# Router parts at two places of a token tile, and list products as one operation a part

## The chip, the cores and the metric

The kernel runs on one core of a Trainium2 chip. TensorE (PE in the profile) multiplies matrices, VectorE (DVE), ScalarE (ACT) and GpSimd (POOL) work on elements, and SyncE (SP) issues most transfers. Each engine runs its own queue of instructions in order and waits on semaphores. The metric is the device time of one execution in microseconds (us); the median of several runs counts.

## The reference

Sliding-window attention is followed by a mixture of experts with one expert a token:

```python
q, k, v: (8, 8, 576, 64); window 64, causal
scores = where(mask, q @ k.T / 8, -1e9)
attn = softmax(scores); x = (attn @ v) as (4608, 512)
do_compute = x @ w_skip > 0
logits = x[do_compute] @ w_gate                 # 8 experts
e = argmax(logits); gate = softmax(logits)[e]
y = gate * (relu(x @ w1[e]) @ w2[e])            # w1 (512, 1024), w2 (1024, 512)
out = x, and x + y where do_compute
```

## The kernel before

The 4608 tokens are 36 tiles of 128. One loop with the tile number t from 0 to 36 runs the attention as a pipeline: in step t TensorE gets the scores of tile t+1 (`ps`), products that prepare the gate (`pw`, `pk`), in steps 32 and 33 the transposes of the first expert's tokens (`px`), then `av` of tile t-2 and the transposes of tile t-1 (`pt`). VectorE does the softmax of tile t (`soften`: `mx`, `s`, and the exponential on ScalarE), then the normalisation of tile t-2 (`tile_out`: `r`, `x`, `lh`; `lh` holds the parts of the gate's logits). ScalarE copies the transposes to `ptm`, which `av` needs. The whole order is written out by hand: each engine takes its instructions in the order in which the code issues them.

The router works on groups of tiles (`GRP`: 8, 8, 6, 8, 4 and 2 tiles). `route` is a generator that issues the work of a group in parts: the logits `lg`, `gmx` and `gd`, `gfi` and `gfm`, `goh` and `gohb` (which expert each token takes, as one-hot rows), then the sums over tokens on TensorE, `pr`, with `gds` and `base` on VectorE, then `gnd`, `gs`, `gate`, `pos`, `low`, `posp`, and on POOL the one-hot rows `hot`. `routes` takes it a part further, so many parts as its first argument says; a part that follows "sums" is held back until it has been asked for three times, and `routes(1, False)` does not issue it. `pt`, `pw`, `pk`, `pr`, `pe` and the experts' `p` share two PSUM buffers of the tag "t".

After 22 tiles (`NCLOSE`) the generator also closes the first lists: `close_first` picks the two experts with the most tokens (`perm`, from which SyncE loads the first weights), `entries` makes the lists of their first tokens, `es0` (`es` in the profile), and POOL gathers those tokens to the four `xg` of the first two experts.

`entries` builds a list as a product of one-hot matrices: for a step of tiles VectorE compares positions (`of`), POOL multiplies the result with five rows of values (`ofv`), TensorE sums over tokens (`pe`, or `peu` for the late lists), and VectorE turns the sums into indices and gates (`raw_e`, then `es0` or `les`).

After the loop the experts run in blocks of products (`p` is a block of 12 with 256 columns, `yw` and `yv` one of 12 with 512) while the last groups are routed. Weights arrive as `raw`, and are split into `whi` (ScalarE) and `wlo` (VectorE); ScalarE and VectorE turn a `p` into `hh` and `hl`. When the router is done, `order_experts` (from `c` on) and `late_lists` make the late lists in nine steps of four tiles; `PACE` says how many parts of `late_lists` are issued before each expert block. From `les` POOL gathers the next tokens (`xg`), which TensorE transposes to `px`, and a finished `yo` goes out by a scatter on POOL.

Of the kernel before, what the change touches and what calls it, by code (L numbers as in the profile page):

```python
# [13 lines left out]
ALU = mybir.AluOpType  # L14
# [5 lines left out]
P = 128  # L20
# [19 lines left out]
NCLOSE = 22  # L40
# [9 lines left out]
USPLIT = (35,)  # L50
RATE = 1

PACE = 4

XSPLIT = (32, 33)

# [68 lines left out]
def window_attention_moe(ctx: ExitStack, tc, a, out):  # L125
    nc = tc.nc
# [26 lines left out]
    vals = const.tile([P, 5, NT], BF16, name="vals")  # L153
# [90 lines left out]
    def soften(t):  # L244
        ps = ss[t]
        s = sp.tile([P, 2 * 4, P], F32, name="s")
        flat = ps.rearrange("p r h k -> p (r h) k")
        mx = sm.tile([P, 8], F32, name="mx", bufs=2)
        nc.vector.tensor_reduce(mx, flat, axis=AX.X, op=ALU.max)  # L249
        nc.vector.tensor_tensor(s, flat, mx.unsqueeze(2).to_broadcast([P, 8, P]), op=ALU.subtract)  # L250
        nc.scalar.activation(s, s, AF.Exp, scale=0.125)  # L251
        ss[t] = s
# [214 lines left out]
    def entries(ts, starts, le, pool, since, take, step, lag):  # L467


        nc_ = starts.shape[1]  # L470
        parts(slice(since, ts.stop))
        yield
        pe, built = None, []
        for t0 in range(ts.start, ts.stop, step):
            m = min(step, ts.stop - t0)
            tj = slice(t0, t0 + m)
            of = pool.tile([P, m, nc_], BF16, name="of", bufs=1 if take is psum else 3)
            nc.vector.tensor_tensor(
                of,
                posp[:, tj].unsqueeze(2).to_broadcast([P, m, nc_]),  # L480
                starts.unsqueeze(1).to_broadcast([P, m, nc_]),
                op=ALU.is_equal,
            )
            ofv = pool.tile([P, m, 5, nc_], BF16, name="ofv", bufs=1 if take is psum else 3)
            for v in range(5):
                nc.gpsimd.tensor_tensor(  # L486
                    ofv[:, :, v], of, vals[:, v, tj].unsqueeze(2).to_broadcast([P, m, nc_]), op=ALU.mult
                )
                if v in (1, 3):
                    yield  # L490
            built.append((t0, ofv))
            yield "sums" if take is psum else None
            if len(built) < lag and t0 + step < ts.stop:
                continue
            if pe is None:
                pe = (
                    psum.tile([P, 5, nc_], F32, name="pe", tag="t", bufs=2, padded_shape=[P, 5, 100])
                    if take is psum
                    else banks["late"].tile([P, 5, nc_], F32, name="peu", tag="u", bufs=1, padded_shape=[P, 5, 100])
                )  # L500
            while built and (len(built) >= lag or t0 + step >= ts.stop):
                first_t, ofs = built.pop(0)
                for j in range(ofs.shape[1]):
                    t = first_t + j
                    nc.tensor.matmul(pe, hot[:, t], ofs[:, j], start=t == ts.start, stop=t == ts.stop - 1)
                yield
        entry(pe, le, pool)
        yield
# [65 lines left out]
    held = [None, 0]  # L574

    def routes(n, sums=True):

        for _ in range(n):
            if not late:
                return  # L580
            if held[0] == "sums":
                held[1] += 1
                if not sums or held[1] < 3:
                    continue
            held[:] = next(late[0], late), 0
            if held[0] is late:
                late.pop(0)
# [52 lines left out]
    def weight_dma_first():  # L640
        weight_dma(ptr["dma"])
        ptr["dma"] += 1
# [189 lines left out]
    with tc.manual_schedule():  # L832
# [35 lines left out]
        for t in range(NT + 1):  # L868
            m, r = divmod(t, 9)
            for f, n in at.get(t, ()):  # L870
                f(n)
            if t + 1 < NT:
                score(t + 1)
            for f, n in gate_at.get(t, ()):
                f(n)
            rest = its[0].split(*xhl[0], XSPLIT.index(t), "t") if t in XSPLIT else None
            routes(1)
            if t < NT:
                soften(t)
            if t >= 2 and t < NT:  # L880
                tile_out(t - 2)
            if rest is not None:
                rest()
            routes(1, False)
            if t >= 1 and t < NT:
                transpose_p(t - 1)
            routes(1 if t < NCLOSE else 2)
            for f, n, j in lower_at.get(t, ()):
                f(n, j)
            for _ in range(U0.count(t)):  # L890
                weight_dma_first()
            if t in USPLIT:
                weight_split(ptr["split"])
                ptr["split"] += 1
# [181 lines left out]
        while True:  # L1076
# [4 lines left out]
            if tabling is not None:  # L1081
                next(tabling, None)
            for _ in range(PACE):
                next(listing, None)
# [92 lines left out]
```

## Time and profile before

| | before |
|---|---|
| median of 3 runs | 467.93 us (466.89 to 470.29) |
| profiled execution | 465.82 us |
| its span in the profile | 464.0 us |
| TensorE busy | 411.8 us (89%) |
| VectorE busy | 308.3 us (66%) |
| ScalarE busy | 218.4 us (47%) |
| POOL busy | 125.6 us (27%) |

The span is the stretch of the trace from the first to the last instruction of the program; the execution's own time is 1.8 us more. The busy shares are means over stages that differ: the attention loop lasts until about 183 us, the experts' products from there to the end.

### The profile page before, as it was taken

What the parts mean: (1) busy time and instruction counts of PE and PEld (TensorE: products, weight loads), DVE (VectorE), ACT (ScalarE), POOL (GpSimd) and SP (SyncE); (2) the same over time, 40 slices, a digit from 0 to 9 for tenths busy, and PEclk for the clock granted to TensorE, in tenths of its full rate; (3) what the DMA queues carried; (4) which work ended last, traced back from release to release, by engine and by line L of the source; (5) the groups of instructions that cost most, each with busy time, mean ns of one, the idle gap of its engine ahead of it and who ended that gap; (6) DMA issues with size and microseconds to landing.
All of it is one profiled execution on the core that took longest, in us unless ns stands there. A gap on an engine that the chain in (4) does not pass through costs nothing.

```text
span 464.0 us, 11417 instructions
## 1 busy us (share of the span) xinstructions
PE 411.8 (89%) x4568; PEld 342.9 (74%) x4568; DVE 308.3 (66%) x609; ACT 218.4 (47%) x365; POOL 125.6 (27%) x188
## 2 busy tenths in 40 slices
PE   2899989979779967894899999999999999999983
PEld 2577767867567756783689888898888789988762
DVE  2478989989788988687533658947355566756420
ACT  1387667767546755462312534434243445444410
POOL 2311215116052505246860402405007030101010
PEclk9999999999898998996999999999999999999998
DMA  7999989949847943556533561845537456656100
GB/s 245 394 351 401 384 284 404 398 127 390 356 146 250 355 128 112 151 196 207 174 111 100 184 207 69 277 137 185 193 114 250 161 197 198 216 193 219 51 29 20
DMA packets 35096, 99.31 MB, mean 214 GB/s; under 512 B 4480, under 2 KB 6528, under 8 KB 35040
## 3 DMA queue, kind: packets, MB, share of 16 engines
q1 hardware_dynamic: 31840, 88.97, 55.8%
q0 software_dynamic: 3200, 9.58, 5.8%
q8 instruction: 37, 0.61, 0.5%
q14 instruction: 19, 0.16, 0.1%
HBM read 84.46 MB, written 14.39 MB: 213 GB/s over the span
## 4 chain that ended last, share of the span: by engine, by line
PE 64%; DVE 9%; ACT 3%; DMA 3%; POOL 2%; issue 1%; POOLq 0%; DVEq 0%; SPq 0%; ACTq 0%
PE p L695 8%; PE p L697 8%; PE p L696 8%; PE av L344 4%; PE yw L695 3%; PE yw L697 3%; PE yw L696 3%; PE yv L695 3%; PE yv L696 3%; PE yv L697 3%; PE pt L260 3%; PE ps L234 3%; POOL ofv L486 2%; DMA vm<-vp 2%; DVE s L250 2%; PE px L684 2%
## 5 line engine op out<-in xcount | busy, mean ns | idle before, releaser
L648 DVE TENSOR_TENSOR wlo<-raw,whi 128x1024 fp32r<-128x1024 f32 x72 | 88.1, 1229 | 15.4 <-ACT whi L647 15.4
L732 ACT ACTIVATE hh<-p 128x256 fp32r<-128x256 f32 (+6 forms) x72 | 27.7, 384 | 146.6 <-PE p L697 145.6
L697 PE MATMUL p<-xh,wlo 128*128 128x256 f32 (+6 forms) x288 | 84.2, 292 | 1.6 <-DVE wlo L648 1.6
L695 PE MATMUL p<-xh,whi 128*128 128x256 f32 (+6 forms) x288 | 85.3, 296 | 0.3 <-ACT ptm L261 0.3
L696 PE MATMUL p<-xl,whi 128*128 128x256 f32 (+6 forms) x288 | 84.1, 292 | 0.0
L733 DVE SCALAR_TENSOR_TENSOR hl<-p,hh 128x256 fp32r<-128x256 f32 (+6 forms) x72 | 30.3, 420 | 76.8 <-ACT hh L732 76.7
L647 ACT CAST whi<-raw 128x1024 fp32r<-128x1024 f32 x72 | 74.2, 1046 | 0.0
L755 POOL DMA_INDIRECT out<-yo,les x18 | 18.9, 1052 | 156.0 <-DVE yo L754 144.1
L695 PEld LDWEIGHTS p<-xh,whi 128*128 128x128 f32 x288 | 55.0, 191 | 3.4 <-ACT ptm L261 0.4
L251 ACT ACTIVATE s<-s 128x1024 f32<-128x1024 f32 x36 | 38.1, 1058 | 40.3 <-DVE s L250 38.1
L697 PEld LDWEIGHTS p<-xh,wlo 128*128 128x128 f32 x288 | 55.1, 191 | 2.0 <-DVE wlo L648 2.0
L696 PEld LDWEIGHTS p<-xl,whi 128*128 128x128 f32 x288 | 55.1, 191 | 1.4
L249 DVE TENSOR_REDUCE mx<-ps 128x8 f32<-128x1024 f32 x36 | 43.8, 1215 | 15.0 <-PE ps L234 15.0
L250 DVE TENSOR_TENSOR s<-ps,mx 128x1024 f32<-128x1024 f32 x36 | 44.1, 1225 | 5.1 <-PE pt L260 0.9
L260 PE MATMUL pt<-ident,s 128*128 128x128 f32 x288 | 41.0, 284 | 5.6 <-ACT ptm L261 5.6
L344 PEld LDWEIGHTS av<-vm,ptm 128*64 128x64 f32 x1024 | 36.1, 138 | 11.4 <-issue 5.7
L344 PE MATMUL av<-vm,ptm 128*64 128x74 f32 x1024 | 41.3, 233 | 2.2 <-ACT ptm L261 2.1
L315 POOL COPY vm<-vm 64x1184 f32<-64x1184 f32 x16 | 18.6, 1168 | 88.5 <-ACT vm L314 61.0
L234 PE MATMUL ps<-k,q 64*64 64x128 f32 x1024 | 37.3, 285 | 4.1 <-DMA q<-qT 4.1
L261 ACT COPY ptm<-pt 128x512 f32<-128x512 f32 x72 | 38.6, 580 | 4.7 <-PE pt L260 4.5
L260 PEld LDWEIGHTS pt<-ident,s 128*128 128x128 f32 x288 | 31.5, 143 | 9.8 <-ACT ptm L261 6.5
L234 PEld LDWEIGHTS ps<-k,q 64*64 64x64 f32 x1024 | 33.1, 142 | 7.2 <-DMA k<-kT 4.4
(173 smaller groups left out, 697.5 us busy)
## 6 DMA issues: line engine op xcount, KB each, us to landing
raw<-wq SPq DMA_DIRECT2D x72, 512.0 KB, 4.4
vm<-vp SPq DMA_DIRECT2D x16, 592.0 KB, 6.8
vT<-vT SPq DMA_DIRECT2D x16, 512.0 KB, 7.6
out<-x SPq DMA_DIRECT2D x32, 256.0 KB, 6.3
q<-qT SPq DMA_DIRECT2D x15, 512.0 KB, 9.0
k<-kT SPq DMA_DIRECT2D x8, 640.0 KB, 6.8
k<-kT SPq DMA_DIRECT2D x7, 512.0 KB, 8.3
kt<-kT SPq DMA_DIRECT2D x8, 256.0 KB, 7.6
```

Of the source, the lines that this page charges most:

```text
L234: nc.tensor.matmul(ps[64 * hf : 64 * hf + 64, r, p], q[h, p], k[h, :, p], start=False, stop=p == 3, skip_group_check=True,)
L249: nc.vector.tensor_reduce(mx, flat, axis=AX.X, op=ALU.max)
L250: nc.vector.tensor_tensor(s, flat, mx.unsqueeze(2).to_broadcast([P, 8, P]), op=ALU.subtract)
L251: nc.scalar.activation(s, s, AF.Exp, scale=0.125)
L260: nc.tensor.transpose(pt[:, p], s[:, 4 * r + p], ident)
L261: nc.scalar.copy(ptm[:, 4 * r : 4 * r + 4], pt)
L344: nc.tensor.matmul(av[64 * hf : 64 * hf + 64, h // 4, (h % 4) * VW : (h % 4 + 1) * VW], ptm[:, (h % 2) * 4 + h // 2, 64 * hf : 64 * hf + 6 ...
L647: nc.scalar.copy(hi, raw)
L648: nc.vector.tensor_tensor(lo, raw, hi.bitcast(F32), op=ALU.subtract)
L695: nc.tensor.matmul(o, lh, rh, start=first, stop=False)
L696: nc.tensor.matmul(o, lh, rl, start=False, stop=False)
L697: nc.tensor.matmul(o, ll, rh, start=False, stop=last)
```

## The change

In the attention loop the router's parts are issued at other places. Before, each step t had one `routes` ahead of the softmax, one (that never issues the sums) behind the normalisation, and one behind the transposes (two from tile 22 on). Now there is one between softmax and normalisation and one behind the transposes, and from tile 22 on one more ahead of the softmax. A held part is issued at the second call instead of the third.

In `entries` the five products of a step, one for each row of values, become one operation with five times as many elements, and the two parts that lay between them are gone. `PACE` goes from 4 to 3.

```diff
--- before.py
+++ after.py
@@ -50,7 +50,7 @@
 USPLIT = (35,)
 RATE = 1
 
-PACE = 4
+PACE = 3
 
 XSPLIT = (32, 33)
 
@@ -482,12 +482,12 @@
                 op=ALU.is_equal,
             )
             ofv = pool.tile([P, m, 5, nc_], BF16, name="ofv", bufs=1 if take is psum else 3)
-            for v in range(5):
-                nc.gpsimd.tensor_tensor(
-                    ofv[:, :, v], of, vals[:, v, tj].unsqueeze(2).to_broadcast([P, m, nc_]), op=ALU.mult
-                )
-                if v in (1, 3):
-                    yield
+            nc.gpsimd.tensor_tensor(
+                ofv,
+                of.unsqueeze(2).to_broadcast([P, m, 5, nc_]),
+                vals[:, :, tj].rearrange("p v t -> p t v").unsqueeze(3).to_broadcast([P, m, 5, nc_]),
+                op=ALU.mult,
+            )
             built.append((t0, ofv))
             yield "sums" if take is psum else None
             if len(built) < lag and t0 + step < ts.stop:
@@ -580,7 +580,7 @@
                 return
             if held[0] == "sums":
                 held[1] += 1
-                if not sums or held[1] < 3:
+                if not sums or held[1] < 2:
                     continue
             held[:] = next(late[0], late), 0
             if held[0] is late:
@@ -874,17 +874,18 @@
             for f, n in gate_at.get(t, ()):
                 f(n)
             rest = its[0].split(*xhl[0], XSPLIT.index(t), "t") if t in XSPLIT else None
-            routes(1)
+            if t >= NCLOSE:
+                routes(1)
             if t < NT:
                 soften(t)
+            routes(1)
             if t >= 2 and t < NT:
                 tile_out(t - 2)
             if rest is not None:
                 rest()
-            routes(1, False)
             if t >= 1 and t < NT:
                 transpose_p(t - 1)
-            routes(1 if t < NCLOSE else 2)
+            routes(1)
             for f, n, j in lower_at.get(t, ()):
                 f(n, j)
             for _ in range(U0.count(t)):
```

The instructions themselves stay the same but for the list products; the order on the engines moves. On TensorE, in the attention loop, the sums `pr` of the first group stand here before (`pw` and `pk` prepare the gate, `av` is the product with the values, `pt` the transposes, `ps` the scores):

```order
L294 MATMUL pw<-vT,wg 32x256 x4
L344 MATMUL av<-vm,ptm 64x74 x16
L260 MATMUL pt<-ident,s 128x128 x8
L410 LDWEIGHTS trib
L410 MATMUL pr<-gohb,trib 128x64
L413 LDWEIGHTS onesb
L413 MATMUL pr<-gohb,onesb 128x64
L413 LDWEIGHTS onesb
L413 MATMUL pr<-gohb,onesb 128x56
```

There they follow the transposes at once. In the changed kernel they stand here on TensorE:

```order
L220 LDWEIGHTS identb
L220 MATMUL ps<-band,identb 64x512
L220 LDWEIGHTS identb
L220 MATMUL ps<-band,identb 64x512
L234 MATMUL ps<-k_112,q 64x128 x16
L302 MATMUL pk<-ident,vw_1014 128x128 x2
L410 LDWEIGHTS trib
L410 MATMUL pr<-gohb,trib 128x64
L413 LDWEIGHTS onesb
L413 MATMUL pr<-gohb,onesb 128x64
```

The sums moved from directly behind the transposes to behind the next tile's scores and `pk`; those of the second and third group move in the same way, and those of the fourth stay directly behind the transposes.

On VectorE, among the first expert blocks, the choice of the experts of the fifth group (four tiles, 32 columns: `gohb`) stood between the first `wlo` and the normalisation of the last tile but one:

```order
L648 TENSOR_TENSOR wlo_134<-raw_128,whi_133 128x1024
L398 SCALAR_TENSOR_TENSOR gfi<-gd,cf 128x32
L400 TENSOR_REDUCE gfm<-gfi 128x4
L405 TENSOR_TENSOR goh<-gfi,gfm 128x32
L407 SCALAR_TENSOR_TENSOR gohb<-lg,goh 128x32
L353 TENSOR_SCALAR r<-av 128x8
L354 RECIPROCAL r<-r 128x8
L355 TENSOR_TENSOR x<-av,r 128x512
L361 TENSOR_TENSOR lh<-av,r 128x8x9
L648 TENSOR_TENSOR wlo_136<-raw_129,whi_135 128x1024
L733 SCALAR_TENSOR_TENSOR hl<-p_3186,hh 128x256
L422 TENSOR_TENSOR gds<-pr,base 128x32
```

All of it was issued before the first `hl` of an expert block. In the changed kernel it stands, on the same engine, behind two `wlo` and the `hl` of the fourth expert block:

```order
L648 TENSOR_TENSOR wlo_3104<-raw_130,whi_3103 128x1024
L648 TENSOR_TENSOR wlo_3106<-raw_131,whi_3105 128x1024
L733 SCALAR_TENSOR_TENSOR hl<-p_3288,hh 128x256
L386 TENSOR_REDUCE lg<-lh 128x36
L393 TENSOR_REDUCE gmx<-lg 128x4
L395 TENSOR_TENSOR gd<-lg,gmx 128x32
L398 SCALAR_TENSOR_TENSOR gfi<-gd,cf 128x32
L400 TENSOR_REDUCE gfm<-gfi 128x4
L405 TENSOR_TENSOR goh<-gfi,gfm 128x32
L407 SCALAR_TENSOR_TENSOR gohb<-lg,goh 128x32
L733 SCALAR_TENSOR_TENSOR hl<-p_3321,hh 128x256
L422 TENSOR_TENSOR gds<-pr,base 128x32
```

All parts of this group moved behind the start of the experts' products; on TensorE its sums stand behind the fifth block of `p` where they stood behind the first. Those of the sixth group (16 columns) stood behind six blocks of `p` and one of `yw`, and stand now behind eight of `p` and one and a half of `yw`.

On VectorE, at the end of the late lists, `raw_e` (which reads the sums of the lists) stood ahead of the two `yo` and of the next `hl`:

```order
L478 TENSOR_TENSOR of<-posp,begins 128x72
L733 SCALAR_TENSOR_TENSOR hl<-p_3710,hh 128x256
L478 TENSOR_TENSOR of<-posp,begins 128x72
L513 COPY raw_e<-peu 128x90
L514 SCALAR_TENSOR_TENSOR raw_e<-raw_e 128x18
L515 TENSOR_SCALAR les<-raw_e 128x18
L516 TENSOR_TENSOR raw_e<-raw_e 128x18
L517 TENSOR_TENSOR les<-raw_e 128x18
L754 SCALAR_TENSOR_TENSOR yo<-yw,es_119,xg_120 128x512
L754 SCALAR_TENSOR_TENSOR yo<-yw,es_119,xg_121 128x512
L733 SCALAR_TENSOR_TENSOR hl<-p_3790,hh 128x256
```

Nothing lay between the last `of` and `raw_e`. In the changed kernel it stands, on the same engine, behind two `yo` and an `hl`:

```order
L648 TENSOR_TENSOR wlo_3108<-raw_132,whi_3107 128x1024
L478 TENSOR_TENSOR of<-posp,begins 128x72 x3
L754 SCALAR_TENSOR_TENSOR yo<-yw,es_119,xg_120 128x512
L754 SCALAR_TENSOR_TENSOR yo<-yw,es_119,xg_121 128x512
L733 SCALAR_TENSOR_TENSOR hl<-p_3729,hh 128x256
L513 COPY raw_e<-peu 128x90
L514 SCALAR_TENSOR_TENSOR raw_e<-raw_e 128x18
L515 TENSOR_SCALAR les<-raw_e 128x18
L516 TENSOR_TENSOR raw_e<-raw_e 128x18
L517 TENSOR_TENSOR les<-raw_e 128x18
L733 SCALAR_TENSOR_TENSOR hl<-p_3756,hh 128x256
```

So `les` comes one expert block later against the last sums; the scatters of the two `yo` stand ahead of the gathers by `les` on POOL, where they stood behind them. The first late sums `peu` on TensorE come two blocks of `p` and one of `yw` later than before, and those of two steps stand there together.

In the attention loop the first lists (`es0`) come out one tile later: ahead of the row maximum of tile 31, where they came ahead of that of tile 30. The transposes `px` that take the first gathered tokens stand in step 32 as before.

## Rows read from the trace of the kernel before

**Rows 1.** Busy time of each engine by stage; then granted clock, DMA share, GB/s.

```profile
14.00:183.00 169.00, 147.74 (x2884) 116.59 (x2876) 143.68 (x306) 109.40 (x191) 50.58 (x79) 0.97 0.83 302
...
209.60:238.00 28.40, 18.32 (x124) 15.70 (x124) 16.79 (x43) 6.14 (x11) 20.93 (x48) 0.82 0.50 158
238.00:456.00 218.00, 215.92 (x1304) 185.42 (x1302) 123.12 (x195) 87.09 (x141) 41.45 (x36) 1.00 0.50 163
```

**Rows 2.** Waits, TensorE and VectorE 10 to 184 us, TensorE 183 to 250.

```profile
PE pr L410 <- ACT ptm L261: 5.3, 3, 3.0
...
DVE gds L422 <- PE pr L413: 3.3, 4, 0.9
...
PE peu L505 <- POOL ofv L486: 9.8, 4, 6.9
```

**Rows 3.** Timeline of VectorE in the attention loop: start, us, operation [idle before].

```profile
123.48 0.21 DVE L422 TENSOR_TENSOR gds<-pr,base 128x48 f32<-128x48 f32 x1 [0.88 <-PE pr L413]
...
127.96 0.17 DVE L353 TENSOR_SCALAR r<-av 128x8 f32<-128x8 f32 x1 [1.43 <-PE av L344]
...
166.78 0.23 DVE L422 TENSOR_TENSOR gds<-pr,base 128x64 f32<-128x64 f32 x1 [0.76 <-PE pr L413]
```

**Rows 4.** Timeline of TensorE: the scores of two tiles.

```profile
123.80 1.92 PE L234 MATMUL ps<-kt,qt 64*64 64x128 f32 x32
...
158.42 1.04 PE L234 MATMUL ps<-k,q 64*64 64x128 f32 x32
```

**Rows 5.** Timelines of POOL, VectorE and TensorE around the first gather.

```profile
150.64 1.25 POOL L524 DMA_INDIRECT xg<-out,es  x1 [6.13 <-DVE raw_e L516]
...
154.46 1.22 DVE L249 TENSOR_REDUCE mx<-ps 128x8 f32<-128x1024 f32 x1
...
160.25 0.66 PE L684 MATMUL px<-ident,xg 128*128 128x128 f32 x4
```

**Rows 6.** DMA issues, 150 to 151.5 us: the gather, us from issue to landing.

```profile
xg<-out,es POOLq DMA_INDIRECT x1, 7.5
```

**Rows 7.** Timeline of VectorE: parts of the router's fifth group.

```profile
180.88 0.45 DVE L386 TENSOR_REDUCE lg<-lh 128x36 f32<-128x288 f32 x1
...
181.59 0.19 DVE L395 TENSOR_TENSOR gd<-lg,gmx 128x32 f32<-128x32 f32 x1
```

**Rows 8.** Timeline of TensorE around the late lists.

```profile
216.74 0.46 PE L505 MATMUL peu<-ofv,hot 128*128 128x90 bf16 x4 [6.91 <-POOL ofv L486]
216.99 0.56 PE L695 MATMUL p<-xh,whi 128*128 128x256 f32 x1
...
219.70 0.52 PE L505 MATMUL peu<-ofv,hot 128*128 128x90 bf16 x4
...
234.52 0.28 PE L695 MATMUL p<-xh,whi 128*128 128x256 f32 x1
...
235.94 0.28 PE L695 MATMUL p<-xh,whi 128*128 128x256 f32 x1
...
237.78 0.63 PE L684 MATMUL px<-ident,xg 128*128 128x128 f32 x4 [0.26 <-DMA xg<-out,les]
```

**Rows 9.** List products: ns min/median/max; then the mean of a smaller product.

```profile
L486 POOL TENSOR_TENSOR ofv<-of,vals x50: 300/307/1357, 141.6 to 232.5; 128x72 bf16<-128x72 bf16 x45, 128x88 bf16<-128x88 bf16 x5
...
L463 POOL TENSOR_TENSOR left<-gate,vals 128x22 f32<-128x22 f32 x1 | 0.2, 233 | 0.1
```

**Rows 10.** Timeline of VectorE around the late lists.

```profile
208.47 0.15 DVE L952 TENSOR_TENSOR c<-base,cf 128x8 f32<-128x8 f32 x1
...
213.27 1.22 DVE L648 TENSOR_TENSOR wlo<-raw,whi 128x1024 fp32r<-128x1024 f32 x1
...
233.25 0.25 DVE L513 COPY raw_e<-peu 128x90 f32<-128x90 f32 x1 [1.93 <-PE peu L505]
...
234.04 0.18 DVE L517 TENSOR_TENSOR les<-raw_e 128x18 f32<-128x18 f32 x1
...
236.56 0.42 DVE L733 SCALAR_TENSOR_TENSOR hl<-p,hh 128x256 fp32r<-128x256 f32 x1 [1.01 <-ACT hh L732]
```

## Prediction

> **What bounds the kernel now.** I read the stages first, then who waits, then the timeline at the places that the change touches. Up to 183 us VectorE is busy 143.68 of 169.00 us and TensorE 147.74; from 238 us on TensorE is busy 215.92 of 218.00 us at full clock [rows 1]. So whatever time is won or lost before 238 us is kept to the end: behind it there is no slack to lose it in. Between them the late lists are built (209.6 to 238 us): TensorE is busy only 18.32 of 28.40 us there, and its granted clock is 0.82 of full speed, a mean over stretches at 2.4 GHz and one below [rows 1]. The change acts on four places: the waits around the router's sums in the attention loop, the first gather, the sums of the last two router groups among the first expert products, and the late lists. Each is priced against the profiled execution (465.82 us); the median of the runs, 467.93 us, lies 2.1 us above it.
>
> **The attention loop: 3.3 us less.** VectorE waits four times for `pr`, 3.3 us in all; TensorE itself waits three times before `pr` for the copy that frees the buffer of the tag that `pr` shares, 5.3 us in all [rows 2]. The 0.76 us at 166.78 is that of the fourth group [rows 3], whose `pr` still stands directly behind the transposes; that stays. The other three (3.3 - 0.76 = 2.55 us) belong to `pr` standing directly behind the transposes, with the scores of the next tile behind it. Now those scores come first and cover the wait of the shared buffer. The worst of them, 3.0 us, also left TensorE slow: the 32 products of the next score took 1.92 us, where 1.04 us is the rule [rows 4], and VectorE then waited 1.43 us for `av` [rows 3]. I take the three waits whole and half of the 1.43 us, since the buffer's wait does not vanish, it moves to `pk` or `pw` ahead of `pr`: -3.3 us. Bounds: -4.0 us (all of it) and -1.0 us, because `pr` now stands ahead of `av`, and a late `gohb` would hold `av` and with it VectorE's next `r`. The group's parts lie further apart in the tiles, but they are as many operations as before.
>
> **The first gather: 1.9 us more.** With one router step a tile fewer, the first lists come out one tile later: `es` stood ahead of the row maximum of tile 30, now it stands ahead of that of tile 31. The gather that follows `es` was issued at 150.64 and landed 7.5 us later [rows 5, 6], at 158.1 us; TensorE took it into `px` at 160.25 without a wait [rows 5]. Tile 30 ended at 154.46 [rows 5]. One tile later the gather is issued at about 154.6 and lands at 162.1 us, 1.9 us after `px` is due, and `px` stands ahead of `av` on TensorE. The queue of `px` has `av`, the transposes and the next scores behind it, so VectorE waits too. Taken: 1.9 us. Bounds: 0 (a landing in 5.6 us) to 3.5 us (tile 30 longer than before by the router parts that move into it).
>
> **Sums of the last two groups: 3.8 us more.** The sums of the fifth group (32 columns) stood behind one expert block; now they stand behind four more, and ahead of them on VectorE is a row: `hl` of one block, two `wlo`, `hl` of the next, then seven small operations from `lg` to `gohb`. A block of 12 products lasts 235.94 - 234.52 = 1.42 us [rows 8]; its `hl` is done 236.56 + 0.42 - 235.94 = 1.04 us after its end [rows 8, 10]; a `wlo` takes 1.22 us [rows 10]; `lg` takes 0.45 us and the next operations follow some 0.22 us apart [rows 7], together about 1.8 us. So `gohb` is ready 1.04 + 2.4 + 0.42 + 1.8 = 5.7 us after the end of the first of these blocks, and TensorE has two blocks, 2.84 us, until it wants it: 2.9 us of wait. If the two `wlo` are done early, it is 1.04 + 1.8 - 1.42 = 1.4 us. I take 1.8 us, nearer to the lower end, since an earlier wait for a `wlo` is part of the longer one and exists today. Those of the sixth group (16 columns) now stand in the middle of a block of `yw`: ahead of `gohb` are an `hl` (1.04), three small operations (0.7), two `wlo` (2.4), another `hl` (0.42) and four small ones (0.8), 5.4 us; TensorE has a `px` (0.6 [rows 8]), a block and half a `yw` block (1.42 each): 3.4 us, so a wait of 2.0 us. Bounds: 0, if the `wlo` run early, to 2.9 us, as in the group before.
>
> **The late lists: 1.6 us more.** First the price of the product itself. One list product of 72 elements takes 0.307 us in the median and up to 1.357 us [rows 9]; a product of 22 elements takes 0.233 us [rows 9]. The 50 elements between cost 0.074 us, 1.5 ns each, so 360 elements come to 0.307 + 288 x 0.0015, some 0.7 us (estimate), between 0.5 us and 1.5 us (five times 0.3). I take 0.7. The Trainium skill, "GPSIMD Engine Reference", § 7 (Performance pitfalls for Q7 kernels), speaks against the single operation: a read whose step exceeds 8 bytes costs about 2.9 cycles an element, and the values are now read across the five planes, 72 bytes apart; by that rule the operation would come to an estimated 0.87 us and the sum to 0.3 us more. No row here has such a read.
>
> In the first wait TensorE stands 6.9 us before the first list products [rows 2, 8]. Today c8 begins at 208.47 and TensorE gets its operand at 216.74 [rows 8, 10]. The way to the `wlo` behind the first `of` is 213.27 - 208.47 = 4.8 us [rows 10]; now one more `wlo` (1.2) stands ahead of `of`, and TensorE wants two lists at once, so two products of 0.7 us, the second perhaps held while a `wlo` runs (up to 1.2 us): 7.4 to 8.6 us. c8 follows the `hl` of the tenth block, 1.04 us after its end, or up to 1.3 us later behind two `wlo`. TensorE has `yw` (2.84, twelve products of twice the width of a block's) and a block (1.42) to do meanwhile. The wait is 4.2 to 6.7 us; I take 5.5: -1.4 us. The other waits for list products (9.8 - 6.9 = 2.9 us, [rows 2]) shrink to 1.0 us, since nine products of 0.7 us replace 45 of 0.3 us, and only the last group of 16 sums has to wait: -1.9 us (0 to -2.9).
>
> Then a wait appears that is not there today. Today `raw_e` follows the last sums at once (233.25), `les` is done at 234.22, and `px` needs the gather's data at 237.78, a wait of 0.26 us [rows 8, 10]: 3.56 us for the gather, with half a `yw` and two blocks as cover. In the new order VectorE has two `yo` and the `hl` of the next block ahead of `raw_e`: 1.42 + 1.04 us, and 0.97 us from `raw_e` to `les`, then the 3.56 us, together 7.0 us; TensorE has two blocks, 2.84 us. The wait is 4.15 us, 3.9 us more than today. POOL's two `yo` scatters now stand ahead of the gathers, and are issued in that time. Last the clock: after the long wait one block took 219.70 - 216.99 = 2.7 us instead of 1.42 [rows 8], and after 3.0 us a score 0.88 us more [rows 4]. The first stays as it is; for the new wait I add 1.0 us (0 to 1.3). Sum here: -1.4 - 1.9 + 3.9 + 1.0 = +1.6 us (-1.7 to +5.1).
>
> Sum: -3.3 + 1.9 + 3.8 + 1.6 = +4.0 us, 469.8 us for an execution like the profiled one, **471.9 us** on the scale of the median (0.9% slower). A measurement of this kernel can tell about 1% from no change.
>
> **The rivals.**
> 1. Not slower: the gather lands in time and the sums are not late. The transfers are thinner one tile later, or earlier tiles end later than I think; from a landing within 5.6 us on, the 1.9 us are gone. With -4.0 in the attention loop, 0 at the gather, 1.4 for the sums, and -2.7 - 2.9 + 3.9 + 0 in the lists the sum is -4.3 us: 463.6 us. For it speaks that TensorE today waits three times in the attention loop for the very copies that the new place covers [rows 2]; against it, that three new waits must all fall at their lower ends.
> 2. Clearly slower: every new wait lowers the clock. A wait of 3.0 us cost 0.88 us in the next score [rows 4]; three new waits of 1.8 to 2.2 us (gather, both sums) would add 3 x 0.9: 474.6 us. It decides if a wait of 2 us is enough to drop the granted clock; the rows show it for 3.0 and 6.9 us only.
> 3. The single product does not save what it seems to: at 1.5 us each, the two products ahead of the first sums take 1.6 us more, and the last group 1.0 us more: 474.5 us. § 8 (Key points) of the same page of the Trainium skill says that POOL shares its way to memory with VectorE and contends with two-input VectorE instructions; the trace agrees, 1.357 us at most against 0.307 us [rows 9], and a long operation would meet a `wlo` more surely.
>
> **How the numbers follow.** The forecast has 0.45 (469 to 475 us; 0.27 of it within 1%, 0.18 above), the first rival 0.32 (0.14 faster by over 1%, 0.18 within), the second 0.18, the third 0.05. So faster 0.14, within 1% 0.45, slower 0.41. The range runs from 464 us, the first rival, to 476.5 us, the second with its bounds; about 0.1 is left out on either side.
>
> **What would show it.** Right, if in the changed kernel: VectorE's waits for `pr` fall below 1 us in sum before 160 us; `px` at the start of tile 32 waits for its gather; `pr` of 32 and 16 columns show waits of about 2 us for `gohb`; the first list sums still wait about 5.5 us; and the `px` that follows them waits about 4 us for `xg`. Wrong, if the first gather has slack, if a list product takes well over 1 us, or if a wait shows between 238 us and the end that is not there today.

## The result, and the profile after

The changed kernel takes 1.0059 times the time of the kernel before (95% interval 1.0036 to 1.0081): medians of 17 runs each are 471.80 and 468.27 us. That is slower by 2 to 4 us, under 1%; 471.9 us had been forecast. One of the 17 runs, of 797 us, was disturbed and counts in no ratio. The profiled execution is the fastest of its 17 (467.95 us, span 466.1 us), and the repeat that stands further down (474.86 us) is longer than the 473.56 us of the longest that counts. The two traces show the two ends, and a figure is safe only where both have it.

The page's line of TensorE and the line of its granted clock (40 slices, tenths):

```profile
PE 414.0 (89%) x4568; PEld 345.3 (74%) x4568; DVE 306.4 (66%) x609; ACT 217.4 (47%) x365; POOL 113.5 (24%) x148
...
PEclk9999999999999988988779999999999999999998
```

The stages of [rows 1] in the changed kernel:

```profile
14.00:183.00 169.00, 151.34 (x2932) 119.81 (x2926) 143.33 (x310) 111.08 (x194) 48.55 (x73) 0.98 0.85 307
...
209.60:238.00 28.40, 17.26 (x108) 14.85 (x106) 18.82 (x47) 7.45 (x11) 14.86 (x14) 0.82 0.47 158
238.00:456.00 218.00, 215.63 (x1295) 185.39 (x1296) 122.73 (x194) 87.10 (x141) 39.82 (x35) 0.99 0.50 161
```

TensorE has got 3.6 us more done by 183 us, and is as busy as before from 238 us on. Between them it is idler and slower than before (busy 17.26 us against 18.32 in the second row, and from 183.1 to 209.6 us 21.65 us at a granted clock of 0.94 against 23.76 us at 1.00). The boundary that matters is its first expert product: 183.11 us in the trace before, 175.32 us now. From there to the end of the span it was 464.0 - 183.11 = 280.9 us, and is 466.1 - 175.32 = 290.8 us. So the loop gains 7.8 us and the rest loses 9.9 us. Waits that answer to [rows 2], with two new ones:

```profile
PE pr L410 <- ACT ptm L261: 1.8, 1, 1.8
...
DVE gds L422 <- PE pr L413: 1.6, 2, 1.0
...
PE peu L505 <- POOL ofv L485: 8.4, 5, 6.5
PE pr L410 <- DVE gohb L407: 4.0, 2, 2.3
PE px L684 <- DMA xg<-out,les: 3.0, 1, 3.0
```

The waits for `ptm` ahead of `pr` fell from 5.3 to 1.8 us, those of `gds` from 3.3 to 1.6 us; those for list products from 9.8 to 8.4 us. New are the waits for `gohb` (4.0 us) and for the second gather (3.0 us). On the timeline of TensorE they stand here (start, duration, operation, idle time before it):

```profile
154.94 0.63 PE L684 MATMUL px<-ident,xg 128*128 128x128 f32 x4 [0.99 <-DMA xg<-out,es]
...
175.32 0.38 PE L695 MATMUL p<-xh,whi 128*128 128x256 f32 x1
...
191.18 0.18 PE L410 MATMUL pr<-gohb,trib 128*128 128x32 bf16 x1 [1.72 <-DVE gohb L407]
...
203.39 0.17 PE L410 MATMUL pr<-gohb,trib 128*128 128x16 bf16 x1 [2.29 <-DVE gohb L407]
...
220.17 0.46 PE L505 MATMUL peu<-ofv,hot 128*128 128x90 bf16 x4 [6.48 <-POOL ofv L485]
...
238.29 1.12 PE L684 MATMUL px<-ident,xg 128*128 128x128 f32 x4 [3.01 <-DMA xg<-out,les]
```

The first row is the first gather's `px`: it waits 0.99 us, where 1.9 us had been foreseen. The last is the `px` behind the late lists. On VectorE `raw_e` stands behind the `hl` of the block that follows the last sums, and `les` ends at 234.86 us, where it ended at 234.22 us [rows 10] in a kernel that had begun its experts 7.8 us later:

```profile
233.56 0.42 DVE L733 SCALAR_TENSOR_TENSOR hl<-p,hh 128x256 fp32r<-128x256 f32 x1 [4.01 <-ACT hh L732]
233.91 0.24 DVE L513 COPY raw_e<-peu 128x90 f32<-128x90 f32 x1
...
234.68 0.18 DVE L517 TENSOR_TENSOR les<-raw_e 128x18 f32<-128x18 f32 x1
```

### The profile page after: what moved, and what is told of

The parts are those of the page before. It is cut to its first block, busy times and chain, and to the rows that moved or that the text cites. A ratio compares the mean times of both kernels' runs of the same rounds, so it can differ in the third digit from the quotient of the medians.

```text
span 466.1 us, 11370 instructions
## 1 busy us (share of the span) xinstructions
PE 414.0 (89%) x4568; PEld 345.3 (74%) x4568; DVE 306.4 (66%) x609; ACT 217.4 (47%) x365; POOL 113.5 (24%) x148
## 3 DMA queue, kind: packets, MB, share of 16 engines
q1 hardware_dynamic: 31840, 88.97, 55.4%
## 4 chain that ended last, share of the span: by engine, by line
PE 52%; DVE 7%; DMA 3%; ACT 2%; issue 2%; POOL 1%; SPq 0%; POOLq 0%; ACTq 0%; DVEq 0%
PE p L695 8%; PE p L697 8%; PE p L696 8%; PE yw L695 4%; PE yw L697 4%; PE yw L696 4%; PE yv L695 3%; PE yv L696 3%; PE yv L697 3%; PE px L684 2%; DVE wlo L648 2%; PE yu L696 2%; PE yu L697 2%; PE yu L695 2%; DMA xg<-out,es 1%
## 5 line engine op out<-in xcount | busy, mean ns | idle before, releaser
L697 PE MATMUL p<-xh,wlo 128*128 128x256 f32 (+6 forms) x288 | 85.7, 298 | 1.4 <-DVE wlo L648 1.4
L695 PE MATMUL p<-xh,whi 128*128 128x256 f32 (+6 forms) x288 | 86.6, 301 | 0.1
L696 PE MATMUL p<-xl,whi 128*128 128x256 f32 (+6 forms) x288 | 85.5, 297 | 0.0
L695 PEld LDWEIGHTS p<-xh,whi 128*128 128x128 f32 x288 | 56.6, 196 | 3.1 <-ACT whi L647 0.2
L697 PEld LDWEIGHTS p<-xh,wlo 128*128 128x128 f32 x288 | 56.6, 197 | 1.8 <-DVE wlo L648 1.8
L696 PEld LDWEIGHTS p<-xl,whi 128*128 128x128 f32 x288 | 56.7, 197 | 1.5
```

The source lines that it names most:

```text
L695: nc.tensor.matmul(o, lh, rh, start=first, stop=False)
L696: nc.tensor.matmul(o, lh, rl, start=False, stop=False)
L697: nc.tensor.matmul(o, ll, rh, start=False, stop=last)
```

## The experiments

Theory 1: the loop gains by the place of the router's parts, and the loss is what its order pushes behind it: the sums of the last groups and the late lists. Theory 2: the loss is the single list product and its pace. (Where an expectation says something else by theory 2, it is the rival that it names there.) Theory 3, added after the first four runs: the loop gains only because router work is pushed behind it, and that is paid back in full.

**e1_lists**: the kernel before with the list products and PACE of the changed one; the loop is as before.

```diff
-PACE = 4
+PACE = 3
-            for v in range(5):
-                nc.gpsimd.tensor_tensor(ofv[:, :, v], of, ...)
-                if v in (1, 3):
-                    yield
+            nc.gpsimd.tensor_tensor(ofv, ...)
```

> The kernel before with only the list products as one operation and PACE 3; the attention loop and its router parts as before. Theory 1 (the changed attention loop gains some 8 us up to the first expert block, and the loss comes from what its order pushes back behind it: the last two groups' sums and the late lists): the first expert block stays at about 183 us, the first list sums still wait 5 to 7 us, but the lists end several expert blocks ahead of the first px that needs them, so that px waits for nothing: 1 to 4 us faster than before. Theory 2 (the loss is the single list product with PACE 3): 2 to 4 us slower than before, with waits for list products above the 9.8 us of before.

Measured: 1.0038 (1.0002 to 1.0074) times before, some 2 us slower: theory 1 had the sign wrong. From the first expert product to the end it takes 472.3 - 189.94 = 282.4 us, as much as the kernel before within the spread of its two traces (280.9 and 282.4 us), and no `px` waits there. What it loses, it loses in the loop. Tiles 22 to 31, from row maximum to row maximum, take 56.2 us, where they take 52.8 and 51.4 us in the two traces of the kernel before. The first lists' parts come out in other tiles there, now that `entries` has fewer of them. VectorE waits at `raw_e`, and 3.54 us at `r` for something that the trace doesn't name, so why it costs so much stays open. Rows of VectorE and TensorE:

```profile
148.46 0.18 DVE L513 COPY raw_e<-pe 128x20 f32<-128x20 f32 x1 [1.14 <-PE pe L505]
...
155.30 0.17 DVE L353 TENSOR_SCALAR r<-av 128x8 f32<-128x8 f32 x1 [3.54 <-remote]
...
189.94 0.39 PE L695 MATMUL p<-xh,whi 128*128 128x256 f32 x1
```

So the list products with PACE 3 bring nothing and take nothing behind the loop; the two were not tried apart here.

**e2_five**: the changed kernel with five products in a row in place of the single one.

```diff
-            nc.gpsimd.tensor_tensor(ofv, ...)
+            for v in range(5):
+                nc.gpsimd.tensor_tensor(ofv[:, :, v], of, ...)
```

> The changed kernel with five list products of 72 elements again in place of each single one, issued as one part with nothing between them. Theory 1: five products take 1.5 us in place of 0.82 us, two steps are needed before the first sums, so TensorE waits 1 to 2 us longer there and up to 1 us longer at the last sums: 1 to 3 us slower than the changed kernel, some 473 us. Theory 2 (a long operation is locked out by VectorE for longer): 1 to 3 us faster than the changed kernel.

Measured: 1.0126 (1.0076 to 1.0175) times before, so slower than the changed kernel by about 0.7%, 3 us, by two ratios from two chips. A step of five products takes 1.36 us where VectorE doesn't disturb it, the single one 0.82 us. The waits for list products grow from 8.4 to 12.1 us:

```profile
PE peu L503 <- POOL ofv L486: 12.1, 6, 7.0
```

Theory 2 falls: in this order the single operation is the better one.

**e4_late**: the changed kernel with more router parts between the first expert blocks; the loop is untouched.

```diff
         transpose_p(NT - 1)
-        routes(1)
+        routes(2)
...
         for _ in range(2):
-            routes(1)
+            routes(3)
...
         while late:
-            routes(2)
+            routes(4)
```

> The changed kernel with more router parts between the first expert blocks (2, 3, 3 and then 4 in place of 1, 1, 1 and then 2). The attention loop is untouched. Theory 1: the first expert block stays at about 175 us; the sums of the fifth and sixth group come earlier and still wait 1 to 3 us each; the late lists begin two blocks earlier and end three blocks ahead of the px that needs them, so its wait of 3.0 us and the low clock behind it vanish: 3 to 7 us faster than the changed kernel, 465 to 469 us. Theory 2: no more than 1 us faster, since the products are the same.

Measured: 0.9799 (0.9752 to 0.9846) times before, 2.0% faster: 462.22 us where the kernel before had 470.75 us on this chip. By the two ratios that is 2.6% faster than the changed kernel, more than expected. From the first expert product to the end it takes 461.8 - 179.02 = 282.8 us, 8 us less than the changed kernel. On TensorE the second wait for `gohb` is down from 2.29 to 0.46 us, the first wait for a list product is what it was, and no `px` waits for its gather:

```profile
179.02 0.58 PE L695 MATMUL p<-xh,whi 128*128 128x256 f32 x1
...
189.12 0.18 PE L410 MATMUL pr<-gohb,trib 128*128 128x32 bf16 x1 [1.73 <-DVE gohb L407]
...
195.78 0.17 PE L410 MATMUL pr<-gohb,trib 128*128 128x16 bf16 x1 [0.46 <-DVE gohb L407]
...
209.38 0.46 PE L505 MATMUL peu<-ofv,hot 128*128 128x90 bf16 x4 [6.49 <-POOL ofv L485]
```

**e6_four_late**: one more part per tile from tile 22 on (as many as before), and four parts per block behind the loop.

```diff
                 transpose_p(t - 1)
-            routes(1)
+            routes(1 if t < NCLOSE else 2)
...
         while late:
-            routes(2)
+            routes(4)
```

> The changed kernel with one more router part behind the transposes from tile 22 on (as many per tile as before) and four parts per expert block behind the loop. Theory 1: the fourth and fifth group's parts go back into the attention loop and cost it 1 to 3 us of its 8 us; nothing of them waits behind it, the lists end early, px waits for nothing: 463 to 467 us, faster than both kernels. Theory 2: about 470 us.

Measured: 1.0094 (1.0058 to 1.0131) times before; the expectation was wrong by some 10 us. The first expert product comes at 186.37 us, later than in any kernel with the changed loop, and the sums of the sixth group wait 4.28 us:

```profile
186.37 0.58 PE L695 MATMUL p<-xh,whi 128*128 128x256 f32 x1
...
200.77 0.17 PE L410 MATMUL pr<-gohb,trib 128*128 128x16 bf16 x1 [4.28 <-DVE gohb L407]
```

Tiles 22 to 31 take 53.5 us here, and 46.7 to 48.0 us in the eight traces of the changed loop. VectorE begins 105 operations in them here, 100 in the changed loop and 107 in the kernel before. So with the shorter holding the loop keeps its gain from tile 22 on only while it is given fewer parts. TensorE also waits 3.8 us for `gohb` just ahead of the first expert product, which no trace of the kernel before shows; e7 comes back to that wait.

**r_before and r_after**: both kernels once more, on one chip, for their traces.

> The kernel before once more, on the chip of this group: how far the same order repeats. Both theories: row maxima of tiles 9 to 27 within 0.1 us of the first trace in their lengths, first expert block within 5 us of 183 us, and the same time from there to the end (281 us, within 1).

> The changed kernel once more, on the same chip: first expert block 7 to 8 us earlier than in the repeat of the kernel before, and 291 us (within 1) from there to the end.

The first expert product in the kernel before:

```profile
184.18 0.39 PE L695 MATMUL p<-xh,whi 128*128 128x256 f32 x1
```

and in the changed one, with the `px` behind the late lists:

```profile
181.02 0.58 PE L695 MATMUL p<-xh,whi 128*128 128x256 f32 x1
...
244.03 1.12 PE L684 MATMUL px<-ident,xg 128*128 128x128 f32 x4 [3.28 <-DMA xg<-out,les]
```

What is lost behind it repeats: 282.4 us (466.6 - 184.18) against 292.1 us (473.1 - 181.02), 9.7 us lost, as in the first pair (9.9 us), though both stretches are just over 1 us longer than expected. The loop repeats less well: it gained 3.2 us here, 7.8 us there, where 7 to 8 us had been expected. In the six other kernels with the changed loop (e2, e3, e4, e8, e9, e10) the first expert product came between 177.9 and 179.1 us. The row maxima show what repeats. Tiles 9 to 21 take 58.7 us in both traces of the kernel before and 55.4 us in nine of the ten with the new places: 3.3 us, to 0.05 us (in e3 tile 16 took 0.6 us more). Behind that the kernel before doesn't repeat to the 0.1 us that was expected: tile 25 took 6.37 us in the first trace and 4.87 us in the second. The prediction put the long score in that tile down to the wait of 3.0 us ahead of it. Two rows of TensorE in the repeat, to be read beside [rows 4], show the same wait and a score that isn't long:

```profile
124.81 0.18 PE L410 MATMUL pr<-gohb,trib 128*128 128x48 bf16 x1 [3.00 <-ACT ptm L261]
...
125.30 1.04 PE L234 MATMUL ps<-kt,qt 64*64 64x128 f32 x32
```

The spread of the two traces of the changed kernel lies ahead of tile 9 (0.9 us), in tiles 32 and 33 (3.5 us; the first gather's `px` waited 0.99 us in one and 1.8 us in the other) and behind them.

**e7_early_only**: the new places up to tile 21 only; from tile 22 on those of the kernel before.

```diff
             if t < NT:
                 soften(t)
-            routes(1)
+            if t < NCLOSE:
+                routes(1)
...
+            if t >= NCLOSE:
+                routes(1, False)
...
-            routes(1)
+            routes(1 if t < NCLOSE else 2)
```

> The changed kernel with the router parts of tiles 22 to 36 at the places and in the number of the kernel before; the new places only up to tile 21, the shorter holding and the single list product everywhere. Theory 1 (the loop gains by the place of the parts, and the loss is that the last groups and the lists come late): tile 22 begins 3.1 us earlier than before, the tiles behind it cost what they cost before, the first expert block comes at 179 to 182 us, and from there to the end it is about 283 us, as in the kernel before with single list products: 463 to 466 us, 2 to 5 us faster than before. Theory 3 (the gain in the loop is work pushed behind it, which is paid back there in full): no faster than before by more than 1 us.

Measured: 0.9988 (0.9957 to 1.0019) times before, no change that could be told (2 us faster to 1 us slower). Theory 1's 463 to 466 us is missed, and theory 3's number is met, but not for its reason: nothing is paid back behind the loop. The 3.3 us of tiles 9 to 21 are there, and behind the loop it takes 464.8 - 185.12 = 279.7 us, the least of all up to here. It is tiles 22 to 35 that lose some 5 us against the kernel before: the first expert product comes at 185.12 us. TensorE waits there for `gohb` and, ahead of the first lists' sums, for `ptm`:

```profile
185.12 0.58 PE L695 MATMUL p<-xh,whi 128*128 128x256 f32 x1
...
PE pr L410 <- DVE gohb L407: 4.0, 1, 4.0
PE pe L505 <- ACT ptm L261: 3.9, 1, 3.9
```

From tile 22 on, e1 has the same places and the same list products as e7, but holds the sums one call longer, and its trace has no wait for `gohb`. So that wait goes with the shorter holding. The new places with the number of parts and the holding of the kernel before were not run.

**e8_late_pace5**: e4_late with PACE 5.

```diff
-PACE = 3
+PACE = 5
```

> The kernel with more router parts between the first expert blocks (e4_late) with PACE 5 in place of 3. Theory 1: the lists were no longer late for px there, so ending them earlier gains nothing at px; the first list sums come one yw block earlier, so the wait before them grows by what they lose in cover (up to 2.8 us) while the later waits (3.0 us) stay or shrink: within 3 us of e4_late, 460 to 465 us. Theory 2 (the pace of the list products is what costs): 3 us or more faster than e4_late.

Measured: 0.9864 (0.9805 to 0.9922) times before, 460.77 us: level with e4_late within the two intervals, as theory 1 had it. The first wait grew to 7.67 us:

```profile
177.92 0.58 PE L695 MATMUL p<-xh,whi 128*128 128x256 f32 x1
...
205.73 0.46 PE L505 MATMUL peu<-ofv,hot 128*128 128x90 bf16 x4 [7.67 <-POOL ofv L485]
```

**e3_pace4**: the changed kernel with PACE 4, and nothing else.

```diff
-PACE = 3
+PACE = 4
```

> The changed kernel with PACE 4 in place of 3 and nothing else: the lists end two expert blocks ahead of the px that needs them, the sums of the last two groups stand where they stand in the changed kernel. Theory 1: the wait of px for its gather (3.0 to 3.3 us) and the low clock behind it vanish, the two waits for gohb (1.7 and 2.3 us) and the first wait for a list product (6 to 7.5 us) stay: 286 to 288 us from the first expert block to the end, where the changed kernel has 291 to 292; 3 to 5 us faster than the changed kernel, 465 to 468 us. Theory 2 (the list products themselves cost): no gain, since they are the same.

Measured: 0.9896 (0.9863 to 0.9930) times before, 466.45 us where the kernel before had 472.15 us on this chip. This one number turns the change from 0.6% slower to 1.0% faster. From the first expert product to the end it takes 465.5 - 179.13 = 286.4 us, 4.4 us less than the changed kernel's first trace and 5.7 us less than its repeat. The waits for `gohb` stay (2.31 us at the second); the `px` behind the lists doesn't wait for its gather any more, and the clock is full behind it (rows of TensorE, then a stretch with clock as the third number from the end):

```profile
179.13 0.58 PE L695 MATMUL p<-xh,whi 128*128 128x256 f32 x1
...
206.97 0.17 PE L410 MATMUL pr<-gohb,trib 128*128 128x16 bf16 x1 [2.31 <-DVE gohb L407]
...
239.25 0.65 PE L684 MATMUL px<-ident,xg 128*128 128x128 f32 x4 [0.62 <-issue]
...
240.00:250.00 10.00, 10.00 (x65) 8.89 (x64) 1.67 (x4) 1.41 (x4) 3.34 (x4) 1.00 0.33 106
```

**e9_late_pace2** and **e10_lag5**: e4_late with PACE 2; e8_late_pace5 with the sums five steps behind the products.

```diff
-PACE = 3
+PACE = 2
```

```diff
-PACE = 3
+PACE = 5
-... NCLOSE, None, NT // 9, 3)
+... NCLOSE, None, NT // 9, 5)
```

The second diff leaves out the buffers that changed with it: five of `ofv` for three, two of `of` and two of `yo` for three each.

> The kernel with more router parts between the first expert blocks (e4_late) with PACE 2 in place of 3: the first list sums stand half a yw block later and want one list in place of two, and the last stand just ahead of two p blocks and a yw block that px needs. Theory 1: the first wait falls from 6.5 us to 4 to 5 us, px waits for nothing: 0 to 3 us faster than e4_late, 279 to 283 us from the first expert block to the end. Theory 2 (an early pace is what counts): 2 us or more slower than e4_late.

> The kernel with more router parts and PACE 5 (e8_late_pace5) with the list sums following five steps behind the products in place of three (five buffers of ofv, two of of, two of yo): the first sums stand one p block later, and two lists are wanted there. Theory 1: the first wait falls from 7.7 us by the block's 1.4 us less the second product's 0.8 us, so to about 7 us: within 2 us of e8_late_pace5, 279 to 282 us from the first expert block to the end. Theory 2 (more products in flight shorten the list stage): 3 us or more faster than e8_late_pace5.

Measured: 0.9850 (0.9802 to 0.9897) and 0.9841 (0.9781 to 0.9900) times before, no better than e4_late. With PACE 2 the first wait grew to 8.30 us where 4 to 5 us had been expected:

```profile
211.94 0.46 PE L505 MATMUL peu<-ofv,hot 128*128 128x90 bf16 x4 [8.30 <-POOL ofv L485]
```

The first `of` stands further back on VectorE too, behind more `wlo` and `hl`, so asking later for the sums wins nothing. With five steps it is 6.14 us. No pace tried got the first wait below 6 us.

## Why the prediction was right, and where it was not

The total was right by luck, through two errors of opposite sign. The loop with its gather was forecast at -1.4 us and the stretch behind it at +5.4 us; the first pair of traces shows -7.8 and +9.9 us, the repeat -3.2 and +9.7 us. The steps one by one, all against the first pair of traces:

**The attention loop: -3.3 us forecast, with the first gather's +1.9 us a net of -1.4 us; -7.8 us measured, -3.2 us in the repeat.** The mechanism that was named is there for two of three groups: TensorE's waits ahead of the `pr` of the first three groups are gone (one of 1.76 us now stands at the fourth), and so are VectorE's at `gds` for the first two. For the third group VectorE still waits 1.00 us, where it waited 0.88 and the forecast had nothing left. The slow score of [rows 4] doesn't come in the changed kernel; but it doesn't come in the repeat of the kernel before either, so the 0.7 us set for it hung on one trace. What failed was to count only waits with a name. In tiles 9 to 21 the two named waits of the first two groups (0.87 and 0.80 us in the trace before) make half of the 3.3 us that repeat. That work was pushed out of these tiles is not the reason: VectorE begins the same 114 operations in them in every trace. These are the stretches in the kernel before and in the changed one (VectorE is the third of the busy times; it reads 115, as an operation that began earlier runs on into the stretch):

```profile
50.26:108.91 58.65, 52.80 (x1111) 42.56 (x1103) 52.99 (x115) 38.03 (x68) 14.70 (x21) 1.00 0.87 318
50.41:105.80 55.39, 53.73 (x1119) 42.34 (x1111) 51.92 (x115) 39.11 (x70) 13.03 (x17) 1.00 0.91 337
```

VectorE's idle time falls by 2.2 us, and the time in which it is busy with the same operations by 1.1 us, so they overlap more. That fits parts that now stand on VectorE between work that doesn't depend on them. In tile 11 of the changed kernel `goh` begins 1.14 us after the beginning of a subtraction of 1.23 us, `r` begins 0.14 us after the beginning of `gohb`, while `gohb`, which needs `goh`, begins 0.25 us after it; in the next tile `gds` waits for nothing:

```profile
61.04 1.23 DVE L250 TENSOR_TENSOR s<-ps,mx 128x1024 f32<-128x1024 f32 x1
62.18 0.21 DVE L405 TENSOR_TENSOR goh<-gfi,gfm 128x64 f32<-128x64 f32 x1
62.43 0.22 DVE L407 SCALAR_TENSOR_TENSOR gohb<-lg,goh 128x64 bf16<-128x64 f32 x1
62.57 0.16 DVE L353 TENSOR_SCALAR r<-av 128x8 f32<-128x8 f32 x1
...
66.24 0.21 DVE L422 TENSOR_TENSOR gds<-pr,base 128x64 f32<-128x64 f32 x1
```

That the order does this is an argument from these rows and not a run of its own. And the prediction said that the group's parts are as many as before. That holds up to tile 21; it missed that those of the last groups leave the loop. Tiles 22 to 31 give 6.1 us of the 7.8 us of the first pair (52.8 against 46.7 us), and VectorE is busy 3.9 us less in them. e6 and e7, which bring the parts back, reach the first expert product at 186.4 and 185.1 us (e4, on the chip of e6, at 179.0), so most of what the loop gains from tile 22 on hangs on that, with the shorter holding at least. There theory 3 is right about the place of the gain, and wrong about the price: in e4_late the same parts behind the loop cost 1.9 us at most (282.8 us against 280.9 us), if they are issued densely enough.

**The first gather: +1.9 us.** Right in kind: `px` waited 0.99 us, and 1.8 us in the repeat; the gather was issued at 148.94 us, 5.7 us earlier than forecast, as the loop was ahead by then, and landed in 5.9 us in the first trace, where 7.5 us were taken from [rows 6]. It is no fixed price: in three of the six other kernels with the changed loop (e4, e9, e10) `px` doesn't wait for it.

**Sums of the last two groups: +3.8 us.** Right: 1.72 and 2.29 us, forecast as 1.8 and 2.0 us, and 1.73 and 2.31 us in the repeat.

**The late lists: +1.6 us.** First wait 6.5 us for 5.5; the others 1.95 us (0.32, 0.73 and twice 0.45) for 1.0; `px` 3.0 us for 4.15. (The upper bound of that sum comes to +5.0, not +5.1.) The product itself takes 0.822 us in the median, not the 0.7 us worked out from smaller ones, one of which was of another type; and three of the ten take 1.80 to 1.93 us, each while a `wlo` ran on VectorE. One of these is the product ahead of the first sums:

```profile
L485 POOL TENSOR_TENSOR ofv<-of,vals x10: 811/822/1932, 145.4 to 229.7; 128x360 bf16<-128x360 bf16 x9, 128x440 bf16<-128x440 bf16 x1
```

Here the Trainium skill, "GPSIMD Engine Reference", § 7 (Performance pitfalls for Q7 kernels), was closer: the prediction's estimate from its rule for reads with a long step was 0.87 us. That is no test of the rule: the innermost step of the values is a broadcast over 18 elements here, the long step comes once in 18, and the rows give some 1.8 ns an element ((0.811 - 0.300) / 288) where the rule's 2.9 cycles were taken as 2.4 ns. e2_five shows that five operations cost more all the same.

**The clock: +1.0 us forecast, 5 us measured.** This is the term that was mis-sized. TensorE's waits of 0.15 us and more behind the first expert product, up to 252 us, sum to 12.7 us before and 17.6 us now, 4.9 us more, where 4.4 us had been forecast (3.8 + 0.6). The other 5.0 us of the 9.9 us are TensorE's own time over the same products: from the first expert product to the end it is busy 258.31 us before and 263.30 us now (259.27 and 264.81 us in the repeats), at a lower clock, the third number from the end:

```profile
183.11:464.00 280.89, 258.31 (x1616) 221.99 (x1612) 161.97 (x302) 107.58 (x174) 71.72 (x97) 0.98 0.49 158
175.32:466.10 290.78, 263.30 (x1615) 226.79 (x1612) 164.85 (x310) 107.77 (x175) 67.47 (x75) 0.96 0.47 153
```

The clock is 0.76 from 176 to 183 us (the first expert block, behind no new wait) and in the stretches below. A clock of 0.76 is a mean over 2.4 GHz and the lower level, 1.2 GHz. Stretches of the changed kernel:

```profile
203.00:210.00 7.00, 6.61 (x36) 5.96 (x36) 2.68 (x15) 1.84 (x3) 2.13 (x7) 0.76 0.30 104
...
231.00:238.00 7.00, 4.29 (x24) 4.08 (x22) 1.62 (x7) 0.77 (x2) 4.28 (x5) 0.76 0.35 116
238.00:245.00 7.00, 6.71 (x33) 5.75 (x33) 0.69 (x1) 0.92 (x2) 2.44 (x3) 0.76 0.38 104
```

and the same stretches of the kernel before:

```profile
203.00:210.00 7.00, 6.83 (x46) 6.10 (x45) 5.90 (x19) 5.96 (x9) 3.93 (x7) 1.00 0.47 159
231.00:238.00 7.00, 6.00 (x45) 5.08 (x44) 2.96 (x11) 0.77 (x2) 4.57 (x9) 1.00 0.16 42
238.00:245.00 7.00, 7.00 (x47) 6.26 (x46) 1.66 (x5) 1.53 (x4) 4.04 (x4) 1.00 0.53 179
```

The lower clock follows the wait of 2.29 us at 203.39 us and stands on both sides of the wait of 3.01 us at 238.29 us. That was the second rival, which had set 2.7 us for it. Its condition, that a wait near 2 us suffices, is met for some of them only: behind 1.72 us at 191.18 us the clock stayed full up to 203 us here, and in the repeat it was 0.83 from 190 to 200 us behind a like wait. Eight traces have this wait of 1.7 us; the clock fell right behind it in six and stayed full in two (the first trace and e9). Four have the wait of 2.3 us, and it fell behind all four. But it stayed full behind the 3.00 us in the repeat of the kernel before. So the length of one wait doesn't settle it.

**What each part costs** can be read from e3 and e4, each set against both traces of the changed kernel: when only the lists end two blocks earlier, 4.4 to 5.7 us of the 9.7 to 9.9 us behind the loop go (e3); when only the last groups are routed more densely, 8.0 to 9.3 us go (e4). That second figure includes lists that end earlier too, so the two don't add up, and the 3.6 us between them is a difference of two kernels and not the price of one part.

## What to carry to other kernels

Moving fill work out of a loop that two engines share paid here only when the work was issued densely enough where it landed: one constant (PACE 4 for 3), or more router parts for a few blocks, turned 0.6% slower into 1 to 2% faster. Before such a move, list for each consumer behind the loop how many blocks of cover it keeps, and price the waits that appear with the slow clock that may follow them: in sum about as much again here, though a single wait may cost nothing of the kind. Read a row on which a price rests in a second trace of the same kernel: the slow score of [rows 4] was gone in the repeat. Where several terms of both signs are of the size of the answer, a right total says little: check each stretch against the trace.

## What the runs showed of the hardware

A list product of 360 elements on POOL takes 0.811 us at least and 1.932 us at most; five of 72 elements take 1.36 us undisturbed. The long ones ran beside a `wlo`, a VectorE subtraction of 1.2 us or more. The lengths of tiles 9 to 21 repeat from trace to trace to 0.02 us in the same order (but for one tile of e3), while whole runs differ by 5 us; the spread lies in other tiles, some of which wait for the first gather, and one of which (tile 25 before) had the lower clock in one trace and not in the other. TensorE's granted clock fell behind single waits of 2.3 and 3.0 us, fell behind a wait of 1.7 us in six of eight traces, and stayed full behind one of 3.00 us. Products at the lower clock cost 5.0 to 5.5 us, as much as the new waits themselves.
